# A gated linear attention and a feed-forward layer on one core: the order searched anew, some transposes moved from TensorE to transposing transfers

## The chip, the core and the metric

The kernel runs on one core of a Trainium2 chip. A core has five engines that work side by side, each through its own list in order: PE (TensorE, matmuls; PEld is its weight load), DVE (VectorE), ACT (ScalarE), POOL (GpSimd) and SP (SyncE), which here issues every transfer between main memory (HBM) and on-chip memory (SBUF). Transfers are carried out by 16 DMA engines. TensorE writes its results to PSUM, eight banks of 512 float32 in each of 128 partitions, and DVE and ACT read them there. Engines wait for each other through semaphores.

The metric is the device time of one execution in microseconds (us), lower is better, as the median of the runs.

## What is computed

```python
# r, k, v, w: [4, 8, 768, 48]   u: [8, 48]
state = zeros(B, H, D, D)
for t in range(S):
    cur = einsum('bhd,bhe->bhde', u * k[t], v[t])
    y[t] = einsum('bhd,bhde->bhe', r[t], state + cur)
    state = w[t][..., None] * state + einsum('bhd,bhe->bhde', k[t], v[t])
x = y.transpose(0, 2, 1, 3).reshape(3072, 384)

h = x @ w_in                                  # 384 -> 1024
e = exp(h - max(h)); sm = e / (sum(e) + 1e-9)
solu = h * sm
ln = (solu - mean(solu)) / sqrt(var(solu) + 1e-6) * g_ln
out = ln @ w_out                              # 1024 -> 384, float32
```

The first half is a recurrence over 768 steps with a decay w per step and channel, for 4 batches and 8 heads of 48 channels. The second half is a feed-forward layer whose hidden vector is multiplied by its own softmax and then normalised.

## The kernel before

**Units.** The time axis is cut into 6 chunks of 128 steps; a unit is one chunk of one batch, all heads: 24 units, numbered chunk first, so units 4c to 4c+3 are chunk c of the four batches. All sums over steps within a chunk become matmuls.

**Stages of one unit i**, with the words that name them in the order:

- LW, LK, LR, LV: SP loads w, k, r and v, each 128 x 8 x 48 float32, 192 KB, into rings of 7 buffers.
- lw (ACT): the logarithm of w. cum (PE): sums of it along the steps, once up to a step and once from it. ex (ACT): exponential of both, in PSUM. kp (DVE): these factors times k and r, as bfloat16, written side by side in a row of 2 x 8 x 64 = 1024.
- krk, krr (PE): four transposes each, so that the channels of two heads lie across the partitions, first for k, then for r; kr (ACT or DVE): the copy of the 128 x 1024 result from PSUM to kr_s.
- M (PE): products of k and r, 8 heads; m (DVE with the mask, or ACT followed by POOL's sel): the copy with the part above the diagonal cleared.
- p, q, qh (POOL), dg (DVE), dv (POOL): the bonus term with u, per head a sum of r k u times v. qh first halves the sum's length. vb casts v to bfloat16.
- Y (PE): attend, that is M times v, and r times the state of the chunks before. With "i" it also adds dv, by a matmul with the identity; with "n" y's copy on DVE adds it. y (ACT or DVE): the copy to bfloat16.
- S (PE), et (ACT), st (DVE): the state for the next chunk. Units of one batch are bound by it: Y and S of unit i need st of unit i-4.
- X (PE): three transposes of y; xT (ACT or DVE): the copy.
- H (PE): the hidden layer, 8 x 3 matmuls with 128 columns, w_in as the stationary side, so that hidden channels lie across the partitions. e (ACT): its exponential. he (DVE): h times e. hq (ACT or DVE): its square. ea (POOL): the sum of e's two halves, in some units.
- Oa, Ob (PE): for each of 8 blocks of hidden channels, he times w_out (385 columns, the last gives the sum of he), e or ea times a column (the sum of e), and hq times a column (the sum of squares). g_ln and the centring are put into w_out at the start (gw, mn, mc, ce).
- sq (ACT), qm (DVE): square of the sums and the variance. lv (ACT): two instructions, Ln and Exp, that make the factor of the norm. o (ACT or DVE): the product with it. out (SP): the store, 192 KB.

**Order.** Everything is laid out by one long string, ORDER (lines 21 to 67). Its words are carried out from first to last; a word is a stage and a unit, and behind a dot stands the engine (a, d, p) or the PSUM bank (0 to 7). The class InOrder makes each engine issue its instructions in just this order, so a waiting instruction holds back everything behind it on its engine, and SP's list of transfers is one such queue. The semaphores follow from which buffers are written and read. The word hot is a run of matmuls on zeros that keeps TensorE's clock up.

The loop at the end of the kernel reads the string:

```python
    for word in ORDER.split():
        word, _, how = word.partition(".")
        name = word.rstrip("0123456789")
        stages[name](int(word[len(name):]), how)
```

Since every instruction is made through the same helper, the profile gives line 86 for nearly all; groups are told apart by the names of the tiles that they write and read.

Of the kernel before, what the change touches and what calls it, by code (L numbers as in the profile page):

```python
# [8 lines left out]
F32 = mybir.dt.float32  # L9
BF16 = mybir.dt.bfloat16  # L10
# [10 lines left out]
ORDER = """  # L21
LW2 LU0 ik0 lw2 hot5.4 cum2.0 LW1 lw1 us0.7 ih0 LW3 lw3 cum3.2 LR2 uc0 ex2 LK2 p2 LV2 vb2.p kp2 hot4.4 krk2.6 krr2
LR1 LK1 cum1.4 LW0 ex1 kp1 kr2.d hot1.0 S2.7 lw0 et2 LV1 vb1.d LW4 st2 p1 q1 hot2.0 krk1.1 krr1 q2 qh2 dg2 LG0
kr1.a M2.4 ex3 hot1.0 M1.6 m1.d dv2 LR0 LK0 p0 q0 cum0.0 ex0 lw4 cum4.6 ex4 kp0 krk0.1 krr0 LR3 gs0.0 gc0 dg1
m2.d Y2.i0 kr0.d LK3 p3 LR4 LV0 vb0.a dg0 dv1 kp3 Y1.i5 hot3.1 krk3.4 krr3 LK4 kp4 M0.2 m0.d krk4.1 y1.a X1.5
krr4 y2.a X2.0 dv0 xT2.d hot1.6 Y0.n7 y0.d kr3.a M3.2 hot1.0 X0.6 S1.4 p4 q3 kr4.a xT1.a xT0.a LI2 LI1 wi1.a
M4.0 m4.a et1 LI0 S0.5 et0 wi0.d m3.d LO1 wi2.p H1.6 e1 gw5.a H2.0 e2 H0.2 LO0 gw2.a q4 qh4 dg4 qh3 dg3 gw4.p
gw7.p LV3 vb3.p dv3 sel4 LW6 e0 gw6.d st1 LV4 vb4.p he1 lw6 dv4 gw1.d LW5 gw0.d gw3.d mn0.4 mc0 ce5.p ce6.p
Y3.i7 ce4.p he2 st0 he0 cum6.0 y3.a ce7.p hot1.5 X3.6 lw5 xT3.a ce3.d LK6 LR6 p6 Y4.n5 LR5 LK5 ce2.d hq0.a ex6
LW7 cum5.2 H3.6 p5 y4.d ex5 ce1.d ce0.d Oa0.5 kp6 krk6.1 krr6 S4.0 hq1.d Oa1.4 kp5 krk5.3 krr5 X4.2 Ob1 e3 he3  # L30
LV5 q6 q5 kr5.d hq2.a et4 st4 M5.6 kr6.a M6.0 xT4.d lw7 cum7.2 hq3.a sq1 m6.a m5.d dg5 vb5.d qm1 dv5 Ob0 ex7 sq0
qm0 S3.7 qh6 LR7 LK7 p7 kp7 et3 lv1 st3 lv0 H4.0 Y5.n6 y5.d LR9 LK8 o1.d e4 krk7.3 krr7 Oa2.2 he4 X5.7 q7 kr7.d
LW9 lw9 o0.a LK9 p9 LW8 lw8 S5.6 et5 cum9.4 ex9 Ob2 sq2 LR8 p8 st5 dg6 kp9 qm2 LV6 xT5.a LV9 vb6.p dv6 sel6
cum8.0 ex8 kp8 hq4.a LV7 LV11 out1 LW10 dg7 vb7.p dv7 Oa3.3 vb9.a lv2 H5.6 e5 M7.4 m7.d he5 q8 krk9.1 LK10 krr9
kr9.a S9.0 et9 Ob3 sq3 st9 q9 qm3 o2.a out0 ea5.p Y6.i5 y6.a LV8 LR10 Y7.n4 y7.d LW11 LW12 krk8.1 M9.6 lw10 lv3
X6.2 xT6.a m9.d o3.a krr8 LV10 out3 out2 kr8.d qh9 dg9 dg8 hq5.d cum10.4 ex10 kp10 S6.0 vb11.d et6 X7.2 xT7.a
st6 p10 vb8.d dv8 dv9 H6.6 e6 he6 H7.2 lw11 e7 he7 M8.4 m8.a Oa5.1 Y9.n0 Ob5 sq5 y9.d cum11.6 ex11 krk10.5 krr10
qm5 kr10.d S7.4 et7 st7 Oa4.3 hq6.d lv5 lw12 o5.a X9.2 sel8 Y8.i0 vb10.p y8.a LK11 LR11 kp11 xT9.d q10 dg10 p11
M10.4 m10.a sel10 S10.1 et10 st10 dv10 S8.0 et8 S11.7 et11 X8.6 xT8.a LK12 LW13 cum12.4 q11 ex12 lw13 st11 st8
Ob4 sq4 qm4 LW14 LR12 kp12 p12 lw14 lv4 o4.a out5 LK13 LV12 LR13 Y10.n2 dg11 y10.d H8.6 e8 krk12.1 krk11.0 krr11  # L40
krr12 kr12.d he8 kr11.a q12 qh12 cum13.4 H9.2 vb12.p S12.1 ex13 p13 q13 ea7.p dg12 kp13 dv11 LW16 LR14 LK14 e9
he9 et12 st12 M12.6 m12.a Oa6.0 X10.5 xT10.a krk13.4 krr13 kr13.a M11.6 m11.d ea8.p dv12 sel12 p14 cum14.2 ex14
q14 out4 Ob6 sq6 hq8.d M13.4 m13.d LV13 hq7.a LW15 lw15 lw16 kp14 vb13.d H10.6 dg13 qm6 LW18 lw18 Y11.n1 y11.d
Oa8.5 LK16 LR15 LR16 LK15 e10 he10 hq9.a krk14.4 Y12.i3 krr14 lv6 qh14 kr14.d p15 ea10.p dv13 LR18 LV14 vb14.p
q15 qh15 LK18 p18 Ob8 sq8 qm8 y12.a S13.2 et13 st13 o6.a lv8 X11.1 xT11.d cum16.6 ex16 X12.3 hq10.d LW19 kp16
Oa9.4 cum15.0 xT12.a Ob9 ex15 kp15 sq9 o8.a dg14 dv14 qm9 M14.2 m14.a sel14 krk16.7 Oa7.6 krr16 kr16.d lv9 o9.d
cum18.0 ex18 kp18 Ob7 LV15 S14.5 et14 st14 krk15.3 krr15 kr15.d LK19 Y13.i2 lw19 cum19.0 krk18.7 p16 q16 vb15.a
S15.4 y13.a sq7 qm7 dg15 X13.5 xT13.d ex19 LR19 kp19 lv7 o7.a q18 krr18 kr18.d H11.2 et15 st15 krk19.5 krr19
kr19.d LW17 lw17 cum17.0 e11 he11 ex17 ea11.p out8 LK17 LR17 p17 kp17 H12.6 e12 he12 hq11.a p19 H13.4 e13 Oa10.3
Y14.n2 M16.0 m16.a dg16 q19 dv15 y14.d ea12.p ea13.p M15.6 m15.d he13 Ob10 sq10 X14.2 out9 Oa11.1 LW20 qm10 lw20  # L50
cum20.6 hq12.d krk17.0 krr17 out6 out7 LV16 vb16.a dv16 xT14.a S16.2 LR20 ex20 LK20 dg18 et16 st16 lv10 o10.a
H14.4 e14 kp20 Ob11 sq11 kr17.d LK23 qm11 lv11 o11.a Oa12.2 krk20.3 krr20 kr20.a he14 sel16 Y16.n7 y16.d Y15.n6
y15.d M19.4 m19.a M18.0 m18.d Ob12 X15.7 xT15.a q17 hq13.d LV19 LW21 LV17 X16.3 xT16.a ea14.p vb19.a M17.4 m17.d
sq12 LK22 out10 qm12 dg17 qh19 vb17.p sel19 p20 hq14.a LW22 LV20 q20 qh20 dv17 M20.0 LV21 m20.d out11 LK21 H15.6
e15 he15 lw22 ea15.p H16.4 LV18 vb18.p dv18 LR21 p21 lw21 Oa14.3 Y17.n1 LR22 LV23 q21 dg19 dv19 Ob14 LR23 p23
p22 e16 he16 lv12 Oa13.0 LW23 o12.a out12 sq14 qm14 hq15.d vb20.a lv14 dg20 dv20 y17.d cum21.6 ex21 Ob13 cum22.4
sq13 ex22 LV22 vb22.p ea16.p o14.d out14 Y18.n2 y18.d Oa15.1 X18.3 qm13 kp22 lv13 xT18.d X17.2 xT17.a kp21 Ob15
sq15 qm15 S18.5 et18 st18 Y19.n4 y19.d lv15 o15.a out15 o13.a krk22.2 S17.3 et17 lw23 H18.6 e18 ea18.p hq16.d
vb21.d st17 Y20.n5 y20.d X19.4 xT19.d krr22 kr22.a H17.0 he18 hq18.d cum23.4 ex23 kp23 Oa16.3 e17 ea17.p he17
krk21.2 krr21 kr21.a H19.6 e19 krk23.5 X20.4 krr23 q22 qh21 vb23.p out13 xT20.a kr23.a he19 Oa18.2 Ob16 sq16  # L60
M21.0 q23 ea19.p qh23 dg22 dv22 m21.a sel21 qm16 lv16 M22.6 hq19.a M23.4 Ob18 sq18 dg21 H20.0 o16.a out16 m22.d
m23.d Oa19.7 Y22.n6 qm18 lv18 hq17.d Ob19 S19.5 dg23 dv23 e20 Oa17.4 y22.d X22.3 he20 et19 st19 xT22.d dv21
Y21.n6 Ob17 y21.d sq19 o18.a sq17 qm17 lv17 Y23.n1 out18 qm19 lv19 X21.0 xT21.d H22.2 o17.a e22 out17 ea20.p
y23.d H21.0 X23.5 xT23.a e21 hq20.d o19.d out19 Oa20.6 he22 hq22.d H23.4 e23 he21 hq21.d Ob20 sq20 qm20 lv20
o20.a out20 ea22.p Oa22.7 ea21.p Oa21.3 he23 hq23.d Ob22 sq22 qm22 lv22 Ob21 sq21 qm21 lv21 o21.d o22.a out22
out21 ea23.p Oa23.2 Ob23 sq23 qm23 lv23 o23.a out23
"""

NIO, NLW, NKP, NWK = 7, 10, 6, 4
# [24 lines left out]
def kernel(  # L94
# [60 lines left out]
    g_rows = consts.tile([KF, 128], F32)  # L155

# [57 lines left out]
    qm_t = ring("qm", NWK, [C, 1], F32)  # L214
    lv_t = ring("lv", NWK, [C, 1], F32)
# [164 lines left out]

    def scores(i, x):
        kr = kr_s[i % NKP]
        m_ps = live[i]["m_ps"] = bank([C, 2, HP, C], F32, x, "m_ps")
        for hp in range(HP):
            for a in range(2):
                rows = slice(64 * a, 64 * a + 64)
                pe.matmul(m_ps[:, a, hp, :], lhsT=kr[rows, hp, :], rhs=kr[rows, HP + hp, :], start=True, stop=True)
# [80 lines left out]

    def hidden(i, x):
        xT = xT_t[i % NWK]  # L470
        h_ps = live[i]["h_ps"] = bank([128, KF, C], F32, x, "h_ps")
        for f in range(KF):
            for j in range(KM):
                pe.matmul(h_ps[:, f, :], lhsT=win_sb[:, j, f * 128:(f + 1) * 128], rhs=xT[:, j, :],
                          start=(j == 0), stop=(j == KM - 1))

    def hidden_exp(i, x):
        act.activation(out=e_t[i % NWK], in_=live[i]["h_ps"], func=EXP)
# [7 lines left out]
    def hidden_mul(i, x):  # L486
        dve.tensor_mul(out=he_t[i % NWK], in0=live[i]["h_ps"], in1=e_t[i % NWK])

    def hidden_square(i, x):
        he, hq = he_t[i % NWK], hq_t[i % NWK]  # L490
        if x == "a":
            act.activation(out=hq, in_=he, func=SQUARE)
        else:
            (dve if x == "d" else pool).tensor_mul(out=hq, in0=he, in1=he)

    def output(i, part):
        L = live[i]
        e, he, hq, o_ps = e_t[i % NWK], he_t[i % NWK], hq_t[i % NWK], L["o_ps"]
        for f in range(part * KF // 2, (part + 1) * KF // 2):
            pe.matmul(o_ps[:, :DM + 1], lhsT=he[:, f, :], rhs=w2[:, f, :], start=(f == 0), stop=False,  # L500
# [16 lines left out]

    def sums(i, x):
        act.activation(out=sq_t[i % NWK], in_=live[i]["o_ps"][:, DM:DM + 2], func=SQUARE)

    def variance(i, x):
        dve.tensor_sub(out=qm_t[i % NWK], in0=live[i]["o_ps"][:, DM + 2:], in1=sq_t[i % NWK][:, 0:1])

    def scale(i, x):
        act.activation(out=lv_t[i % NWK], in_=sq_t[i % NWK][:, 1:2], func=LN, scale=1e-6 * DF * DF,
                       bias=qm_t[i % NWK])
        act.activation(out=rs_t[i % NWK], in_=lv_t[i % NWK], func=EXP, scale=-0.5)
# [8 lines left out]
    def store(i, x):  # L536
# [11 lines left out]
        sq=sums, qm=variance, lv=scale, o=scaled_out, out=store,  # L548
# [35 lines left out]
```

## Time and profile before

| | us |
|---|---|
| median of 3 runs (155.18 to 155.82) | 155.33 |
| span of the profiled execution, first to last instruction | 152.4 |
| PE busy, 2093 matmuls | 136.4 |
| DVE busy, 227 instructions | 131.8 |
| ACT busy, 247 instructions | 120.0 |
| POOL busy, 149 instructions | 119.0 |

The span leaves out what lies before the first and behind the last instruction, 2.9 us against the median. 27.06 MB go through the DMA engines. The largest groups of the page (engine, operation, written tile <- read tiles, shape, count | busy us, mean ns of one):

| group | count | busy us | mean ns |
|---|---|---|---|
| PE, ps<-w,he, 385 columns (Oa, Ob) | 192 | 44.5 | 325 |
| PE, ps<-xT,win_sb, 128 columns (H) | 576 | 35.5 | 219 |
| PE, ps<-one_col,hq, 1 column (Oa, Ob) | 192 | 31.5 | 164 |
| PE, ps<-ident,kp, 128 columns (krk, krr) | 192 | 16.5 | 227 |
| PE, ps<-ident,y, 128 columns (X) | 72 | 7.6 | 219 |
| DVE, he<-ps,e, 128 x 1024 | 24 | 29.1 | 1214 |
| DVE, hq<-he, 128 x 1024 | 15 | 13.4 | 890 |
| ACT, hq<-he, 128 x 1024 | 9 | 9.5 | 1055 |
| ACT, kr<-ps, 128 x 1024 | 11 | 11.1 | 1012 |
| DVE, kr<-ps, 128 x 1024 | 13 | 8.9 | 682 |
| POOL, ea<-e, 128 x 512 | 17 | 20.0 | 1181 |

A matmul's shown length runs from its start to its modelled end, and the next one starts well before that; the price of one in a row of many is the step from start to start. The same holds for the busy time of PE: it counts the stretches in which at least one is under way.

### The profile page before, as it was taken

The page shows a single profiled execution, that of the slowest core. Times are in us where ns is not written, and L with a number is a line of the kernel's source. Part 1 is how long each engine was busy: PE and PEld are TensorE (multiplying, and loading weights), DVE is VectorE, ACT ScalarE, POOL GpSimd, SP SyncE. Part 2 cuts the span into 40 slices and gives each one's busy share as a digit, 9 for nine tenths or more (in the row PEclk, how much of TensorE's full clock was granted, in tenths as well). Part 3 has the DMA queues.
Part 4 walks back from the last instruction along what each step waited for, and adds up shares of the span by engine and source line. Part 5 has one row for each costly group of instructions (what it writes and reads, how often), then busy time and mean ns, then how long its engine had stood idle before and what let it go on. Part 6 is the DMA issues. An engine that isn't in the chain of part 4 may idle for free.

```text
span 152.4 us, 5172 instructions
## 1 busy us (share of the span) xinstructions
PE 136.4 (90%) x2093; PEld 105.5 (69%) x2093; DVE 131.8 (87%) x227; ACT 120.0 (79%) x247; POOL 119.0 (78%) x149
## 2 busy tenths in 40 slices
PE   6777598968999999999998999999799999999970
PEld 1242365936778889779776689887686988889740
DVE  5029968899999999998999999999999999988940
ACT  4526648869888999799998889998988789938661
POOL 7268986799909994899999997799889979973600
PEclk9959969999999999999999999999999999999998
DMA  3999999989979999989897989995998110112023
GB/s 76 218 216 211 217 334 377 254 175 223 216 151 216 220 204 229 206 177 224 194 203 144 228 195 275 199 199 136 241 205 210 63 45 4 44 63 103 4 79 127
DMA packets 104825, 27.06 MB, mean 178 GB/s; under 512 B 100314, under 2 KB 104419, under 8 KB 104803
## 3 DMA queue, kind: packets, MB, share of 16 engines
q1 hardware_dynamic: 104802, 26.75, 77.4%
q8 instruction: 16, 0.26, 0.7%
q14 instruction: 7, 0.05, 0.1%
HBM read 22.03 MB, written 4.72 MB: 176 GB/s over the span
## 4 chain that ended last, share of the span: by engine, by line
PE 53%; DVE 23%; SPq 8%; ACT 6%; issue 3%; DMA 2%; POOL 1%; DVEq 0%; POOLq 0%
PE ps L86 53%; SPq L86 7%; DVE he L86 6%; DVE m L86 4%; DVE kp L86 4%; DVE w L86 3%; DMA kr_in<-in_k_dram 2%; DVE kr L86 1%; DVE hq L86 1%; DVE y L86 1%; DVE st L86 1%; ACT ps L86 1%; ACT o L86 1%; DVE dg L86 1%; ACT win_sb L86 1%
## 5 line engine op out<-in xcount | busy, mean ns | idle before, releaser
L86 PE MATMUL ps<-w,he 128*128 128x385 bf16 x192 | 44.5, 325 | 1.0 <-DVE w L86 0.7
L86 PE MATMUL ps<-xT,win_sb 128*128 128x128 bf16 x576 | 35.5, 219 | 1.1 <-DVE qm L86 0.8
L86 PEld LDWEIGHTS <-win_sb 128*128 128x128 bf16 x576 | 32.8, 98 | 2.2 <-DVE m L86 0.9
L86 PE MATMUL ps<-one_col,hq 128*128 128x1 bf16 x192 | 31.5, 164 | 0.0
L86 DVE TENSOR_TENSOR he<-ps,e 128x1024 bf16<-128x1024 f32 x24 | 29.1, 1214 | 1.6 <-ACT e L86 1.6
L86 DVE TENSOR_TENSOR kp<-ps,kr_in 128x768 bf16<-128x768 f32 x24 | 22.8, 951 | 7.7 <-DMA kr_in<-in_k_dram 4.9
L86 POOL TENSOR_TENSOR p<-kr_in 128x384 bf16<-128x384 f32 x24 | 24.7, 1038 | 4.5 <-DMA kr_in<-in_k_dram 4.2
L86 POOL TENSOR_TENSOR dv<-vb,dg 128x384 bf16<-128x384 bf16 x24 | 21.7, 907 | 7.5 <-DVE qm L86 3.6
L86 ACT ACTIVATE e<-ps 128x1024 bf16<-128x1024 f32 x24 | 24.5, 1021 | 3.1 <-PE ps L86 2.0
L86 POOL TENSOR_TENSOR ea<-e 128x512 bf16<-128x512 bf16 x17 | 20.0, 1181 | 6.4 <-ACT e L86 5.7
L86 POOL TENSOR_TENSOR q<-p,u_bc 128x384 bf16<-128x384 bf16 x24 | 22.2, 931 | 2.4 <-DVE dg L86 1.7
L86 ACT ACTIVATE ps<-ps 128x768 f32<-128x768 f32 x24 | 19.1, 799 | 5.1 <-PE ps L86 4.3
L86 PEld LDWEIGHTS <-kp 128*128 128x128 bf16 x272 | 17.5, 100 | 6.0 <-DVE kp L86 3.2
L86 PEld LDWEIGHTS <-he 128*128 128x128 bf16 x192 | 18.4, 96 | 4.0
L86 PEld LDWEIGHTS <-hq 128*128 128x128 bf16 x192 | 15.4, 96 | 8.3
L86 DVE TENSOR_TENSOR m<-ps,keep 128x1024 bf16<-128x1024 f32 x15 | 18.2, 1216 | 1.2 <-PE ps L86 1.0
L86 PE MATMUL ps<-ident,kp 128*128 128x128 bf16 x192 | 16.5, 227 | 1.6 <-POOL p L86 1.1
L86 DVE TENSOR_TENSOR hq<-he 128x1024 bf16<-128x1024 bf16 x15 | 13.4, 890 | 0.1
L86 ACT COPY kr<-ps 128x1024 bf16<-128x1024 bf16 x11 | 11.1, 1012 | 2.4 <-PE ps L86 2.4
L86 ACT ACTIVATE lw<-w_in 128x384 bf16<-128x384 f32 x23 | 11.7, 523 | 1.3 <-DMA w_in<-in_w_dram 1.3
L86 PEld LDWEIGHTS <-kr 64*128 64x128 bf16 (+1 forms) x272 | 10.2, 95 | 3.1 <-ACT kr L86 0.7
L86 PE MATMUL ps<-inv_col,ea 128*128 128x1 bf16 x68 | 11.2, 165 | 0.0
(90 smaller groups left out, 293.7 us busy)
## 6 DMA issues: line engine op xcount, KB each, us to landing
w_in<-in_w_dram SPq DMA_DIRECT2D x24, 192.0 KB, 3.7
kr_in<-in_r_dram SPq DMA_DIRECT2D x24, 192.0 KB, 3.7
kr_in<-in_k_dram SPq DMA_DIRECT2D x24, 192.0 KB, 3.7
v_in<-in_v_dram SPq DMA_DIRECT2D x24, 192.0 KB, 3.6
out_dram<-o SPq DMA_DIRECT2D x24, 192.0 KB, 2.6
win_f<-in_moe_w_in_dram SPq DMA_DIRECT2D x3, 512.0 KB, 6.4
wout_f<-in_moe_w_out_dram SPq DMA_DIRECT2D x2, 768.0 KB, 9.0
u_row<-in_u_dram SPq DMA_DIRECT2D x1, 1.5 KB
```

Source lines behind the costliest of these rows:

```text
L86: made = make(*args, **kwargs)
```

## The change

The string ORDER is replaced as a whole: the order of all stages, the engine of those that can run on two, and the PSUM banks are other ones. Three stages get a second form, and one is split:

- In units 14 and 16 to 23, krk, krr and kr are replaced by kt: one transfer, issued by SP, that turns the 128 x 1024 row block of kp into kr_s.
- In units 12, 16 and 18 to 23, X and xT are replaced by xt, which turns y (128 x 384) into xT.
- In units 12, 14, 16 to 19, 21 and 23, H is computed the other way round, with xT as the stationary side and 512 columns of w_in at a time, so that the steps lie across the partitions. The sum of e and the sum of squares then come from the ACTIVATEs that make e and hq, as sums along the row, and Oa and Ob hold the 385-column matmuls alone. he is written to one of four buffers in the space of the float32 w_in, and ht turns it (128 x 1024) by a transfer into the form that Oa needs. sv squares the sum of e; the scale in lv changes since the sum is no longer divided by the root of 1024.
- lv is Ln alone, and Exp becomes a word of its own, rs.

Counts that change, before and after: krk and krr 24 and 15; X 24 and 16; hq on ACT 9 and 19, on DVE 15 and 5; kr on ACT 11 and 6, on DVE 13 and 9; xT on ACT 15 and 12, on DVE 9 and 4; y on ACT 7 and 2, on DVE 17 and 22; attend with dv by matmul 7 and 2; ea 17 and 11; qh 12 and 8; o on ACT 19 and 16, on DVE 5 and 8; sel 9 and 10; vb on ACT 6 and 7, on DVE 6 and 3, on POOL 12 and 14. Of the weights' preparation, one cast of w_in moves from DVE to ACT, two gains move from DVE to ACT and one centring from DVE to POOL. The warm-up runs go from 19 matmuls to 37: 13 at the start, three times 4, 2, and 10 ahead of M1.

In the new string SP's list begins LW1 LW2 LV0 LK2 LW0 LR0 LK1 LR1 LK0; the weights LI and LO stand behind 26 loads (18 before), and its last part reads: kt21 kt20 xt19 LR22 LK22 ht14 out9 kt23 ht12 out11 LV21 kt22 xt16 out13 LV23 xt18 out8 LV22 ht17 out15 xt21 LV20 ht19 xt23 ht16 ht18 out12 out14 xt22 xt20 ht21 ht23, then the last eight stores.

```diff
+    ht_t = [win_f.rearrange("p a n -> p (a n)")[:, j * DF // 2:(j + 1) * DF // 2].bitcast(BF16) for j in range(NHT)]
...
+    def turned_kr(i, x):
+        sp.dma_start_transpose(out=kr_s[i % NKP], in_=kp_t[i % NKP].rearrange("t a h d -> t (a h d)"))
+
+    def turned_x(i, x):
+        sp.dma_start_transpose(out=xT_t[i % NWK], in_=y_t[i % NWK])
+
+    def turned_he(i, x):
+        sp.dma_start_transpose(out=he_t[i % NWK], in_=ht_t[i % NHT])
...
+    by_rows = {int(word[2:].split(".")[0]) for word in ORDER.split() if word.startswith("ht")}
+
     def hidden(i, x):
         xT = xT_t[i % NWK]
+        if i in by_rows:
+            h_ps = live[i]["h_ps"] = bank([C, 2, 512], F32, x, "h_ps")
+            for j in range(KM):
+                for n in range(2):
+                    pe.matmul(h_ps[:, n, :], lhsT=xT[:, j, :], rhs=win_sb[:, j, n * 512:(n + 1) * 512],
+                              start=(j == 0), stop=(j == KM - 1))
+            return
...
     def hidden_exp(i, x):
+        if i in by_rows:
+            act.activation(out=flat(e_t[i % NWK]), in_=flat(live[i]["h_ps"]), func=EXP, accum_out=be_t[i % NWK])
+            return
...
     def hidden_mul(i, x):
+        if i in by_rows:
+            dve.tensor_mul(out=ht_t[i % NHT], in0=flat(live[i]["h_ps"]), in1=flat(e_t[i % NWK]))
+            return
...
     def hidden_square(i, x):
         he, hq = he_t[i % NWK], hq_t[i % NWK]
-        if x == "a":
+        if i in by_rows:
+            act.activation(out=flat(hq), in_=ht_t[i % NHT], func=SQUARE, accum_out=s2_t[i % NWK])
+        elif x == "a":
...
         for f in range(part * KF // 2, (part + 1) * KF // 2):
+            if i in by_rows:
+                pe.matmul(o_ps[:, :DM + 1], lhsT=he[:, f, :], rhs=w2[:, f, :], start=(f == 0), stop=(f == KF - 1))
+                continue
...
+    def spread(i, x):
+        act.activation(out=sq_t[i % NWK][:, 1:2], in_=be_t[i % NWK], func=SQUARE)
...
     def scale(i, x):
-        act.activation(out=lv_t[i % NWK], in_=sq_t[i % NWK][:, 1:2], func=LN, scale=1e-6 * DF * DF,
-                       bias=qm_t[i % NWK])
+        act.activation(out=lv_t[i % NWK], in_=sq_t[i % NWK][:, 1:2], func=LN,
+                       scale=1e-6 * DF if i in by_rows else 1e-6 * DF * DF, bias=qm_t[i % NWK])
+
+    def root(i, x):
         act.activation(out=rs_t[i % NWK], in_=lv_t[i % NWK], func=EXP, scale=-0.5)
```

## The prediction, made before the changed kernel was built or run

> **What bounds the kernel now.** I read four views, in this order: the busy times and the chain of waits, to find the engine that sets the end; the windows, stage by stage; the timeline of TensorE, for the price of each step; and the transfers after 118 us, for the room that the new ones would use.
>
> ```profile
> span 152.4 us, 5172 instructions
> PE 136.4 (90%) x2093; PEld 105.5 (69%) x2093; DVE 131.8 (87%) x227; ACT 120.0 (79%) x247; POOL 119.0 (78%) x149
> ...
> 43.27 31.86 PE ps L86 x551
> ...
> 83.53 6.06 PE ps L86 x79
> ...
> 110.34 37.23 PE ps L86 x601
> ```
>
> The last three rows are pieces of the chain (start, length, what). From 43 to 75 us and from 110 us to the end TensorE sets the time without a gap; between 75 and 110 us the chain hops mostly between DVE instructions. So two engines bind in turn. The windows (columns: engine busy, granted clock, share of the 16 DMA engines, GB/s) show who stands close behind:
>
> ```profile
> 43.30:75.10 31.80, 31.80 (x554) 26.39 (x554) 30.82 (x54) 29.30 (x66) 26.20 (x32) 1.00 0.96 204
> 75.10:110.30 35.20, 33.67 (x563) 27.39 (x560) 34.63 (x54) 32.27 (x67) 32.98 (x35) 1.00 0.95 201
> 110.30:147.60 37.30, 37.23 (x601) 30.14 (x601) 33.97 (x58) 28.90 (x68) 27.52 (x30) 1.00 0.30 82
> ```
>
> The DMA engines are full (0.95) until the last load has gone and nearly empty (0.30) in the stretch that TensorE alone decides. ACT has 8.4 us of room there, DVE 3.3 us. The prices on TensorE come from starts, since a matmul's shown length includes its pipeline:
>
> ```profile
> 119.83 1.50 PE L86 MATMUL ps<-xT,win_sb 128*128 128x128 bf16 x24
> 121.17 0.33 PE L86 MATMUL ps<-st,kr 128*128 128x96 bf16 x4
> ...
> 121.55 0.33 PE L86 MATMUL ps<-ident,y 128*128 128x128 bf16 x3
> 121.72 0.39 PE L86 MATMUL ps<-ident,kp 128*128 128x128 bf16 x4
> 121.94 1.50 PE L86 MATMUL ps<-xT,win_sb 128*128 128x128 bf16 x24
> ...
> 123.75 0.33 PE L86 MATMUL ps<-w,he 128*128 128x385 bf16 x1
> 123.92 0.17 PE L86 MATMUL ps<-inv_col,ea 128*128 128x1 bf16 x1
> 123.95 0.16 PE L86 MATMUL ps<-one_col,hq 128*128 128x1 bf16 x1
> 123.97 0.32 PE L86 MATMUL ps<-w,he 128*128 128x385 bf16 x1
> ```
>
> The hidden product (H) takes 121.17-119.83 = 1.34 us, the three transposes of y (X) 0.17 us, four of k or r 0.22 us (eight: 0.45 us), a 385-column matmul 0.17 us and each one-column matmul behind it 0.025 us: the next 385-column one starts 0.22 us after the last, 0.05 us of it for two of them.
>
> **The change on TensorE.** Nine units lose krk and krr: 9 x 0.45 = 4.1 us. Eight lose X: 8 x 0.17 = 1.4 us. Eight compute H by rows and lose the eight hq and four ea columns of the output product: 12 x 0.025 = 0.30 us; their six 512-column matmuls pass the same 3,072 columns as the 24 of 128 did, at 0.165/385 us a column 1.30 us, 0.04 us less; together 8 x 0.34 = 2.7 us. The matmul that adds dv inside attend goes from 7 units to 2: 5 x 0.165 = 0.8 us. Units that sum e by eight columns instead of ea's four go from 7 to 5: 0.2 us. Sum: 9.2 us less, nearly all in units 12 to 23, where TensorE sets the end.
>
> Warm-up matmuls go from 19 to 37. TensorE's other work starts as loads arrive (busy 33.7 of the first 43.3 us), so I cost the 18 at nothing; if that cover fails, the ten ahead of M1 cost 10 x 0.22 to 0.43 = 2 to 4 us (0.43 us is the step of the first four, 1.91/4 with the last one's pipeline off).
>
> **On the other engines,** by the rows' means. DVE: ten hq fewer (890 ns), four kr (682), five xT (349), one m, three vb (635), one win_sb, two gains, one centring less; five y (551) and three o (610) more, four sums over 384 instead of 192 columns: -14.0 us, to about 118. ACT: ten hq more (1,055 ns: +10.6), five kr (1,012: -5.1), three xT (-1.4), five y (-2.4) and three o (-1.7) less, one m, one vb, one win_sb and two gains more (+3.7), eight 1-column squares (sv, 170 ns: +1.4). Sixteen ACTIVATEs also give a sum along the row, which no row shows: between nothing and one smallest instruction (170 ns) each, 0 to 2.7 us, and I take 1.6, nearer the middle. ACT: +6.7, to about 127. POOL: six ea (1,181) and four halvings (548) less, one mask, two casts, one centring more: -6, to 113. Ln and Exp apart change no duration: back to back they stood 0.03 us apart (148.00 + 0.30, then 148.32), so at most 24 x 0.03 us of ACT, nothing on the path.
>
> So TensorE 127, ACT 127, DVE 118: three near-equal engines, all at work in order. **How much of 9.2 us arrives?** In the stretch 75 to 110 us, where three engines were near full together, TensorE lost 35.20-33.67 = 1.5 us, 4.3%. I expect that loss over the 75 us or so in which they now run together: 3.3 us. It is an estimate; its bounds are 0 (43 to 75 us: no loss) and 7 us (double).
>
> **The transfers** are the unknown. 25 enter SP's queue: 17 of 256 KB (nine of kp, eight of he) and eight of 96 KB (y), and each waits in the queue for DVE or ACT to have written its source. Behind kt14 stand three loads of units 16 and 18; behind kt19, 16, 17 and 18 the stores out6, out7, out4 and the loads of v19 and w23; behind xt19 the loads of k and r of unit 22; behind xt21 that of v20, which POOL needs for vb20 and dv20, so Y20 waits for it. The room:
>
> ```profile
> DMA  0001900000000000060023004700000140083600
> ...
> out_dram<-o SPq DMA_DIRECT2D x10, 192.0 KB, 1.8
> ```
>
> These are the transfers from 118 us on: an almost empty machine, and a 192 KB store lands 1.8 us after its issue. No row shows a transposing transfer. By engine time: the loads move 192-byte pieces, 104,802 packets for 77.4% of 16 x 152.4 us, so 18.0 ns each; a 128 x 1024 tile turned in runs of 128 elements (256 B) is 1,024 such pieces, 64 per engine: 1.15 us. Low end, at the rate of the store: 0.7 us. High end, if one is wholly done before the next begins, at the loads' 3.7 us for 192 KB: 4.9 us. I take 1.15 us, the row with the nearest piece size, and 1.8 + 1.15 = 3 us to land.
>
> The Trainium skill, "DMA: Bandwidth & Descriptors", section "Latency and other measured facts", gives 261 GB/s for a transposing transfer; by that a 256 KB one takes 1.0 us and the sum is the same. Against the change speaks "VectorE: DVE Perf Modes", section "The three transpose paths": 1,309 ns by transfer for 128 x 128 against 390 ns on TensorE; the trace's 55 ns steps there are far below its 390, and eight blocks one after the other would take 10.5 us, beyond my high end.
>
> Where they fall: from ht14 on, the order lists ten large and six small ones, seven stores and four loads ahead of the last (ht23), and 23.5 us of TensorE work at the prices above. A small one counts 0.375 of a large, a plain issue 0.39 us: 12.25 x 1.15 + 4.3 = 18.4 us. It fits, with 5 us to spare. It ceases to fit at (23.5-4.3)/12.25 = 1.6 us each.
>
> **Forecast.** 152.4 - 9.2 + 3.3 = 146.5 us of span; the 2.9 us between the span and the median of the runs (155.33) stay: 149.4, say 149.5 us; own range 147.5 to 152.
>
> **Rivals.**
> A. Everything arrives: no loss by crowding, 152.4 - 9.2 + 2.9 = 146.1 us. For: 43 to 75 us ran without a gap. Against: ACT now has as much work as TensorE.
> B. ACT becomes the bound: it was 28.3 of the first 43.3 us at work; with 127 us in all, 15 lost at the start and 3.6 at the end the span is 145.6 at best, a median of 148.5, and at 95% in between 152.3, a median of 155.2; the upper part, 153 to 156, is this rival. For: hq goes to it. Against: its work is spread more evenly.
> C. Late loads: those behind waiting transposes come late for the last attends, 2 to 5 us: 151.5 to 154.5. For: the four v loads stand among the last ten transposes. Against: the DMA engines are idle there.
> D. The other side: transposes run one behind the other, in SP's queue or in the engines, and TensorE waits at the late M, H and Oa. Each large one costs x; the end slips by 12.25x + 4.3 - 23.5 us. It decides from x = 2.0 us (slip 5.8, the gain gone); at x = 3.0, midway between my value and the high end, the slip is 17.5: 167 us; at 4.9, 40.8: 190 us. For: plain issues already hold SP for 0.4 to 1.0 us under load, and between ht23's issue and Oa23 there are only 2.7 us of TensorE work, less than my 3 us to land. Against: stores of nearly that size land in 1.8 us. The skill's 1,309 ns a block would be beyond even 190.
> E. That the turned units' work isn't less on TensorE I give nothing: the instructions are gone from the code.
>
> **Chances.** Forecast 0.44, A 0.11, B 0.12, C 0.03, D 0.30 (0.06 of it at the far end). A measurement of this kernel tells about 0.5% (0.8 us) from no change. Faster: 0.44 + 0.11 + 0.05 of B + 0.02 of C = 0.62. Within 0.5%: 0.05 of B + 0.01 of C = 0.06. Slower: 0.30 + 0.02 of B = 0.32. Range 145.5 to 166: the top is D with x = 2.9; left out are 0.03 below and some 0.15 of D.
>
> **What would show it.** TensorE busy near 127 plus 4 to 7 us of warm-ups; ACT near 127, DVE near 118; kp transposes x120 instead of x192. Transposing transfers landing within 3 to 4 us, SP's waits no longer than now, and TensorE without gaps from 45 us on confirm the forecast. It is wrong if rows such as "PE waits for DMA kr, xT or he" hold more than 3 us, if the interval between successive transposes in SP's queue is above 1.6 us where their sources were long ready, or if ACT stands in the chain for more than a tenth of the span.

## The result and the profile after

The changed kernel takes 167.69 us (median of 4 runs, 165.03 to 168.37) against 155.25 us for the kernel before in runs beside it (154.22 to 155.82). Executions of one kernel fall into a faster and a slower state, and all times and ratios from here on are those of the fast runs, for the changed kernel 166.22 us, 1.0719 times as long as the kernel before, with a 95% interval of 1.0609 to 1.0829. It is slower, and above the top of the predicted range (166 us). The profiled execution took 167.97 us, its span 165.8 us.

The page of the changed kernel: busy times, DMA row (40 slices of 4.1 us), the queue of the transfers, and the shares of the chain of waits.

```profile
span 165.8 us, 4574 instructions
PE 133.9 (81%) x1756; PEld 94.8 (57%) x1762; DVE 118.8 (72%) x208; ACT 123.0 (74%) x270; POOL 110.2 (66%) x143
...
DMA  5999999998989997997999989998989978895443
...
q1 hardware_dynamic: 126082, 32.00, 91.9%
...
DMA 30%; SPq 19%; PE 16%; ACT 15%; issue 8%; POOL 7%; DVE 2%; DVEq 0%; POOLq 0%; ACTq 0%
```

TensorE, DVE and POOL have less to do than before, ACT has 3.0 us more, and the span is 13.4 us longer. The DMA row no longer falls at three quarters of the span: the DMA engines stay nearly full to 149 us. TensorE's share of the chain is 16% (before 53%); DMA and SP's queue have 49% (before 10%). Total time of the 16 DMA engines, from the share of the queue: before 77.4% of 152.4 = 118.0 us, now 91.9% of 165.8 = 152.4 us.

The windows of the changed kernel, with the same limits as those shown of before (columns: engine busy, granted clock, DMA share, GB/s):

```profile
43.30:75.10 31.80, 28.11 (x459) 23.12 (x457) 29.11 (x46) 27.72 (x57) 26.73 (x30) 1.00 0.94 193
75.10:110.30 35.20, 31.26 (x505) 23.75 (x506) 28.31 (x46) 29.99 (x67) 33.03 (x39) 0.97 1.04 197
110.30:147.60 37.30, 30.33 (x340) 19.05 (x343) 26.40 (x44) 29.87 (x75) 18.78 (x23) 0.99 0.96 181
```

In the last stretch the DMA share went from 0.30 to 0.96, and TensorE from 37.2 us busy to 30.3. It is no longer the engine that decides there, and nothing on ACT or DVE is full either.

The transfers of the changed kernel (tile views: the time for which SP's queue holds one, lowest, median, highest in ns; when the first and last are issued), then its transfer view from 118 us on (KB, median us from issue to landing):

```profile
L84 SPq DMA_TRANSPOSE kr<-kp x9: 1305/1828/2499, 77.4 to 128.3; - x9
...
L84 SPq DMA_TRANSPOSE he<-win_f x8: 1248/1258/2527, 122.1 to 151.7; - x8
...
L84 SPq DMA_TRANSPOSE xT<-y x8: 1182/1210/1613, 112.0 to 149.0; - x8
```

```profile
DMA  9963999998974777992993909923998003814080
...
out_dram<-o SPq DMA_DIRECT2D x15, 192.0 KB, 2.2
v_in<-in_v_dram SPq DMA_DIRECT2D x4, 192.0 KB, 3.4
...
he<-win_f SPq DMA_TRANSPOSE x8, 3.1
xT<-y SPq DMA_TRANSPOSE x7, 2.4
kr<-kp SPq DMA_TRANSPOSE x4, 4.5
```

The k and r transfers begin at 77 us, far ahead of the "almost empty machine" that the prediction showed for 118 us on, and that machine is no longer empty: loads of v are still among them. SP's queue in the changed kernel (start, length, what; the length of a row of several includes the gaps):

```profile
95.15 0.70 SPq L84 DMA_DIRECT2D w_in<-in_w_dram  x1
...
99.72 7.35 SPq L84 DMA_TRANSPOSE kr<-kp  x4
107.16 1.50 SPq L84 DMA_DIRECT2D out_dram<-o  x3
108.72 0.45 SPq L84 DMA_DIRECT2D v_in<-in_v_dram  x1
...
115.59 3.85 SPq L84 DMA_TRANSPOSE kr<-kp  x2
...
139.34 0.57 SPq L84 DMA_DIRECT2D v_in<-in_v_dram  x1
```

The row at 95.15 us is the 81st of the 96 loads. Up to there the changed kernel is not behind: in the kernel before, the 81st load's issue ends at 97.2 us. The issue of the last load ends at 139.9 us instead of 115.2. So the 15 last loads take 44 us where they took 18. Between them stand eight k and r transfers, five of y and three of he, 11 large and 5 small ones.

That alone does not make the transfers the cause. In no_turns, the changed order without any of them (an experiment below), the same 15 loads take 41 us, from the end of the first of these two issues to the end of the second:

```profile
93.44 0.82 SPq L84 DMA_DIRECT2D w_in<-in_w_dram  x1
...
135.05 0.43 SPq L84 DMA_DIRECT2D v_in<-in_v_dram  x1
```

SP's queue stands still there in front of stores whose source is not written yet. So the late places of the last loads belong to the new order; what differs is how full the DMA engines are meanwhile and who waits. The longest waits for transfers in the changed kernel (engine, tile, releaser: us in total, times, longest), and then POOL's wait for v in no_turns:

```profile
POOL vb L84 <- DMA v_in<-in_v_dram: 16.6, 9, 2.9
...
PEld L84 <- DMA he<-win_f: 5.8, 4, 2.2
PE ps L84 <- DMA he<-win_f: 4.0, 3, 1.8
```

```profile
POOL vb L84 <- DMA v_in<-in_v_dram: 3.5, 3, 2.9
```

From 60 us on POOL waits 13.7 us for v in the changed kernel and 0.4 us in no_turns. (DVE's wait for r, 9.1 us in all, and ACT's for w, 6.7 us, lie ahead of 60 us but for 0.9 us each, and stand in no_turns too, with 8.3 and 5.1 us.) TensorE's matmuls wait 4.0 us for he, and 2.0 us once for kr; the row of PEld shows the same waits for he at the weight load, so the two don't add up. What TensorE loses to late loads of v reaches it through POOL.

The chain of waits that ended last (start, length, what) has 16.1 us of landings of transposing transfers behind 100 us, and 3.3 us of a load's:

```profile
102.01 5.06 DMA kr<-kp
...
121.47 3.32 DMA kr_in<-in_k_dram
...
135.81 3.54 DMA he<-win_f
...
140.01 3.25 DMA he<-win_f
...
144.02 4.21 DMA he<-win_f
```

To follow the time, I split the span into TensorE's work without warm-ups and the rest (waiting and warm-ups), by the windows 0 to 50, 50 to 100, 100 us to the end. The warm-ups (ps<-warm rows) take 7.8 us of busy time before and 10.9 after.

| us | work 0-50 | 50-100 | 100-end | sum | rest 0-50 | 50-100 | 100-end | sum |
|---|---|---|---|---|---|---|---|---|
| before | 32.6 | 49.2 | 46.8 | 128.6 | 17.4 | 0.8 | 5.6 | 23.8 |
| after | 27.6 | 46.1 | 49.4 | 123.1 | 22.4 | 3.9 | 16.4 | 42.7 |
| after_half | 30.1 | 50.0 | 43.0 | 123.1 | 19.9 | 0.0 | 10.2 | 30.1 |
| no_turns | 27.6 | 47.7 | 58.2 | 133.5 | 22.4 | 2.3 | 10.6 | 35.3 |

(after_half and no_turns are experiments, below.) TensorE did lose 5.5 us of work. The rest grew by 18.9 us: 5.0 at the start, 3.1 in the middle, 10.8 at the end. Of that, 11.5 us (5.0, 1.5 and 5.0) stand in no_turns as well, without a transfer.

### The profile page after: what moved, and what is told of

It is laid out like the page before. It is cut to its first block, busy times and chain, and to the rows that moved or that the text cites. A ratio compares the mean times of both kernels' runs of the same rounds, so it can differ in the third digit from the quotient of the medians.

```text
span 165.8 us, 4574 instructions
## 1 busy us (share of the span) xinstructions
PE 133.9 (81%) x1756; PEld 94.8 (57%) x1762; DVE 118.8 (72%) x208; ACT 123.0 (74%) x270; POOL 110.2 (66%) x143
## 3 DMA queue, kind: packets, MB, share of 16 engines
q1 hardware_dynamic: 126082, 32.00, 91.9%
## 4 chain that ended last, share of the span: by engine, by line
DMA 30%; SPq 19%; PE 16%; ACT 15%; issue 8%; POOL 7%; DVE 2%; DVEq 0%; POOLq 0%; ACTq 0%
SPq L84 18%; PE ps L84 16%; DMA he<-win_f 7%; DMA w_in<-in_w_dram 5%; DMA kr_in<-in_k_dram 5%; ACT e L84 4%; DMA win_f<-in_moe_w_in_dram 3%; DMA kr<-kp 3%; DMA v_in<-in_v_dram 3%; DMA out_dram<-o 2%; DMA kr_in<-in_r_dram 2%; ACT ps L84 2%; POOL m L84 2%; POOL q L84 2%; ACT lw L84 2%
## 5 line engine op out<-in xcount | busy, mean ns | idle before, releaser
L84 PE MATMUL ps<-xT,win_sb 128*128 128x128 bf16 x384 | 23.3, 219 | 2.3 <-DVE kp L84 1.8
L84 PEld LDWEIGHTS <-win_sb 128*128 128x128 bf16 x384 | 22.1, 98 | 3.4 <-issue 2.1
L84 PE MATMUL ps<-one_col,hq 128*128 128x1 bf16 x128 | 21.0, 164 | 0.0
L84 POOL TENSOR_TENSOR dv<-vb,dg 128x384 bf16<-128x384 bf16 x24 | 19.9, 832 | 1.7 <-DVE dg L84 0.8
L84 DVE TENSOR_TENSOR he<-ps,e 128x1024 bf16<-128x1024 f32 x16 | 19.3, 1218 | 1.9 <-ACT e L84 1.2
L84 POOL TENSOR_TENSOR ea<-e 128x512 bf16<-128x512 bf16 x11 | 12.7, 1157 | 10.0 <-ACT e L84 10.0
L84 POOL CAST vb<-v_in 128x384 bf16<-128x384 f32 x14 | 7.1, 505 | 16.7 <-DMA v_in<-in_v_dram 16.6
L84 DVE TENSOR_TENSOR st<-ps,et 128x384 bf16<-128x384 f32 x20 | 10.9, 550 | 4.2 <-ACT et L84 4.0
L84 DVE TENSOR_TENSOR y<-ps,dv 128x384 bf16<-128x384 f32 x22 | 12.0, 549 | 2.5 <-PE ps L84 2.0
L84 PE MATMUL ps<-ident,kp 128*128 128x128 bf16 x120 | 11.3, 240 | 3.0 <-DVE kp L84 2.1
L84 PEld LDWEIGHTS <-hq 128*128 128x128 bf16 x128 | 10.4, 96 | 5.7 <-issue 0.2
```

What stands on the lines that cost most here:

```text
L84: made = make(*args, **kwargs)
```

## The experiments

All ratios are to the kernel before, run beside on the same chip, with the 95% interval.

### Undoing the transfers, one kind at a time and all

no_turns puts TensorE's transposes back for all 25; no_kt, no_xt and no_ht undo only those of k and r, of y, or of he. The order of all else stays.

```diff
-kt14
+krk14.2 krr14 kr14.a
...
-xt12
+X12.1 xT12.a
...
-ht14
-sv14
```

> All 25 transposing transfers are undone in the changed order (krk, krr, kr, X, xT, and H by columns again; the copies go to ACT and DVE in turn). Theory 1 (two losses: before 100 us the new order stands about 8 to 10 us of TensorE work behind, and after 100 us the transposes on SP's queue cost the rest): 158 to 163 us. Rival 2 (the transposes are the whole loss): 153 to 157 us. Rival 3 (the order alone is the loss, the transposes gain what was hoped): 172 us or more.

> Only the nine kt are undone (17.6 us of SP's time in the profile, at 1.3 to 2.5 us each, six of them ahead of loads). Theory 1: the largest part of what the transposes cost is here, since loads stand behind them: 161 to 164 us. Rival 2: 158 to 161 us. Rival 3: 170 us, as TensorE gets 4 us more.

> Only the eight xt are undone (about 10 us of SP's time at 1.2 us each, for 1.4 us of TensorE work). If SP's time per transfer whatever its size is what counts, this helps nearly as much per transfer as undoing ht: 162 to 165 us. If bytes in the DMA engines count, it helps little: 165 to 167 us.

> Only the eight ht are undone (about 11 us of SP's time, 8 x 256 KB, 2.7 us of TensorE work). TensorE waits 10 us for their landing in the profile. Theory 1: 161 to 165 us. Rival 3: 168 us or more.

| | median us | ratio |
|---|---|---|
| changed kernel | 166.22 | 1.0719 (1.0609 to 1.0829) |
| no_kt | 163.93 | 1.0543 (1.0452 to 1.0633) |
| no_xt | 162.94 | 1.0485 (1.0400 to 1.0571) |
| no_ht | 165.42 | 1.0638 (1.0538 to 1.0738) |
| no_turns | 171.15 | 1.1026 (1.0955 to 1.1096) |

Without one kind the kernel is 0.8 to 3.3 us faster (only no_xt's interval stands clear of the changed kernel's), without all three 4.9 us slower. Of the three expectations for no_turns the first two failed by 8 us or more; 171 us is nearest to the third, that the order alone is the loss and the transfers gain. In this order they do gain, 4.9 us on balance. The parts don't add up, as if they shared something, and what is taken out of it first helps until another bound is reached. The window of no_turns shows that other bound:

```profile
100.00:168.80 68.80, 58.20 (x922) 47.29 (x921) 44.84 (x77) 48.70 (x108) 28.77 (x35) 0.97 0.33 89
```

The DMA share is 0.33, close to the 0.30 before the change, and TensorE has 58 us of work left at 100 us. The transfers remove 133.5-123.1 = 10.4 us of TensorE's work from this order and return 42.7-35.3 = 7.4 us of it as waiting. And the changed order without any transfer is 16 us slower than the order before. It may have been made for units that are cheap on TensorE late; no run shows that, and how far my places for the restored stages add to these 16 us isn't known.

### Lighter loads

after_half and before_half load four of the eight heads for units 7 and up. The other heads keep what the buffer held, so the output is no longer the layer's. All instructions of the other engines stay. If the transfers' trouble is that they share the DMA engines with the loads, it should go.

```diff
+    def loaded(i):
+        return H if i < NIO else H // 2
...
-        sp.dma_start(out=w_t[i % NIO][:, :, :D], in_=rows_of(w, i))
+        sp.dma_start(out=w_t[i % NIO][:, :loaded(i), :D], in_=rows_of(w, i)[:, :loaded(i), :])
```

> The changed kernel, but from unit 7 on each load of w, k, r and v brings 4 of the 8 heads (the other half stays what the buffer held), so 6.7 MB less go through the DMA engines and every instruction stays. Theory 1a (the DMA engines are full, loads and transposes land late): the 3 us lost between 50 and 100 us and most of the 11 us lost after it come back, 152 to 157 us. Theory 1b (SP's issue time per transposing transfer, 1.2 us whatever its size, holds the queue): 162 us or more. The start (5 us) stays lost in both.

> The same cut of the loads in the kernel before, as the control: its TensorE has no gaps after 43 us, so 153 to 155 us under every theory; a gain of over 3 us would say that the loads bound it too.

The changed order falls from 166.22 to 153.59 us (0.9948, 0.9900 to 0.9996); the order before doesn't gain, with 155.47 us (1.0077, 1.0045 to 1.0109). The kernel before wasn't held up by the size of its loads, the changed one is, by 12.6 us. Windows of after_half:

```profile
50.00:100.00 50.00, 50.00 (x869) 40.55 (x865) 48.12 (x81) 48.92 (x108) 48.75 (x58) 1.00 0.67 133
100.00:153.20 53.20, 42.98 (x469) 27.83 (x466) 36.26 (x60) 39.50 (x107) 25.16 (x30) 0.96 0.71 153
```

From 50 to 100 us TensorE now works without a gap, as the forecast had it from 45 us on. no_turns_half then took the transfers out with the loads light as well:

> The changed order with all transposing transfers undone, as in no_turns (171.2 us), and the loads halved from unit 7 on. If the order without the transfers is held by loads: 160 us or less. If it is held by TensorE's work and the places at which the undone stages stand: 166 us or more, that is, the transfers were worth their TensorE time to this order and only the DMA engines spoil it.

It takes 168.77 us (1.0882, 1.0828 to 1.0937). So light loads are worth 171.15-168.77 = 2.4 us where no transfer competes and 166.22-153.59 = 12.6 us where 25 do. With light loads the transfers save 168.77-153.59 = 15.2 us, with full ones 4.9. The 10.2 us between are what loads and transfers cost together in this order, but not all of it is shown to be the sharing of the engines. By the table after_half has done 6.4 us more of TensorE's work by 100 us (80.1 against 73.7), and up to 99 us the changed kernel has issued a single transposing transfer, kt14. And no_turns has 10.4 us more work for TensorE, behind which late loads can hide.

### Smaller transfers

In after_small each transposing transfer turns only 128 columns (32 KB) of its tile; the rest of its target keeps old values.

```diff
-        sp.dma_start_transpose(out=he_t[i % NWK], in_=ht_t[i % NHT])
+        sp.dma_start_transpose(out=he_t[i % NWK][:, 0, :], in_=ht_t[i % NHT][:, :C])
```

> The changed kernel, but each of the 25 transposing transfers turns only 128 of its columns (the rest of its target keeps old data), an eighth or a third of the bytes; waits and order stay. Theory 1a: the 33 us that the transposes take of the engines go, 156 to 160 us. Theory 1b: SP still needs about 1.2 us for each, 164 us or more.

> The changed kernel with both cuts: half the bytes of the loads from unit 7 on, and 128 columns for each transposing transfer. after_half was 154.6 us, with TensorE still waiting 9 us for the landing of he. If that rest is bandwidth: 149 to 152 us, near the forecast. If it is the time of a transfer to land, which depends little on its size (2.3 against 2.7 us), or the order itself: 153 to 155 us.

after_small takes 159.53 us (1.0331, 1.0267 to 1.0394): 6.7 us less than the changed kernel. The number of transfers and their places in SP's queue are the same, and SP holds a small one of he nearly as long as a large one (tile view and transfer view of after_small):

```profile
L83 SPq DMA_TRANSPOSE he<-win_f x8: 1172/1184/1682, 119.3 to 146.1; - x8
```

```profile
he<-win_f SPq DMA_TRANSPOSE x8, 2.3
```

1.18 us at 32 KB against 1.26 us at 256 KB. All 25 hold SP for 35.3 us against 38.7, 3.4 us less, while the 16 DMA engines' time for them falls from 34.4 to 4.3 us (76.3% of a span of 160.3 us, less 118.0). So most of the 6.7 us is the time in the DMA engines, not SP's. With the loads light too, after_half_small takes 153.78 us (0.9894, 0.9823 to 0.9965) against after_half's 153.59: where the engines have room, the size hardly matters, and of the 3.1 us that he takes to land 2.3 are there at 32 KB too.

### A transfer that nobody waits for, early and late

before_spare_mid adds to the kernel before nine transfers of 256 KB between the 60th and the 92nd load. They turn a tile that was long ready into space that nobody reads, so that no engine's work and no wait for data changes. before_spare_tail has the same nine behind the last load.

```diff
+    def turned_spare(i, x):
+        into = spare[:, (1 + i % 5) * DF:(2 + i % 5) * DF].rearrange("p (a n) -> p a n", a=KF)
+        sp.dma_start_transpose(out=into, in_=win_sb[:, 0, :])
```

> The kernel before, with nine extra transposing transfers of 256 KB (a fixed tile into the unused w_in buffer, nothing waits for them) behind the loads no. 60, 64, ... 92, where the DMA engines are 0.95 busy. No work of an engine changes. If the engines' time is the price (1.7 us each by the packets of the changed kernel): the loads end about 15 us later and the kernel takes 162 to 170 us. If only SP's issue counts and has room: 156 us or less.

> The kernel before with nine extra transposing transfers of 256 KB as in before_spare_mid, but all behind the last load (one behind v22's load, two each behind H17, H19, H20 and H22). If a transposing transfer costs nothing where the DMA engines and SP are idle: 154 to 155.5 us, against 163.5 us in the full stretch. If it disturbs TensorE's or DVE's memory accesses: 157 us or more.

Early they cost 9.1 us: 163.51 us (1.0583, 1.0542 to 1.0624). Late they cost nothing: 154.80 us (0.9992, 0.9955 to 1.0030). The queue of before_spare_mid, and that of before_spare_tail (packets, MB, share of 16 engines' span):

```profile
span 162.6 us, 5179 instructions
...
q1 hardware_dynamic: 114306, 29.11, 82.2%
```

```profile
span 153.4 us, 5182 instructions
...
q1 hardware_dynamic: 114306, 29.11, 86.7%
```

82.2% of 162.6 less the 118.0 us of the kernel before is 15.7 us, 1.74 us for each; 86.7% of 153.4 gives 15.0 and 1.67. In the changed kernel it is (152.4-118.0)/20 = 1.72 us, a small one counted 0.375. Three runs give one price, half as much again as the 1.15 us that I took. But the price alone decides nothing: paid in the full stretch it delays the loads behind it (the last one goes out at 126.6 us instead of 114.8, and the engines' share is 1.0 until then), paid behind the last load it is free. SP holds each of the nine for 1.4 to 3.6 us in before_spare_mid, so this run by itself doesn't tell SP's time from the engines'; after_small does.

### The order before, with as many transfers as it bears

Transfers in place of TensorE's transposes where the order before has them: four (kt21, kt22, xt19, xt20, all behind the last load), six (with ht17 and ht20), eight (with xt17 and ht16, these two ahead of late loads).

```diff
-X19.4 xT19.d
+xt19
...
-krk21.2 krr21 kr21.a
+kt21
```

> The order before, with four transposing transfers that all stand behind the last load in SP's queue: kt 21 and 22, xt 19 and 20. TensorE loses 0.9 + 0.34 = 1.2 us, ACT two copies of kr. In before_turns8 the transfer of he16 held v22's load back by 4.6 us. If that hold in SP's queue was the harm there: 153 to 154.5 us. If a transposing transfer costs by itself: 155.5 us or more.

> The order before with six turned stages behind the last load: kt 21 and 22, xt 19 and 20, ht 17 and 20. TensorE loses 0.9 + 0.34 + 0.68 = 1.9 us, ACT gains two squares, two reads of the sum and two sv (2 x 1.7 us) and loses two copies of kr (2 us), DVE loses two squares. If TensorE's work is all that counts in that stretch: 152.5 to 153.5 us. If the landing of 2.7 us stands ahead of Oa20 (4.8 us between source and use) or ACT's work holds it: 154 to 155.5 us.

> The order before, with eight transposing transfers where SP and the DMA engines are idle and at least 4.8 us lie between source and use: kt 21 and 22, xt 17, 19 and 20, ht 16, 17 and 20, each issued right behind its source. TensorE loses 2 x 0.45 + 3 x 0.17 + 3 x 0.34 = 2.4 us in the stretch that it bounds alone. If transposing transfers are harmless where the queue is free: 152.5 to 153.5 us. If they cost by themselves: 155 us or more.

| | median us | ratio |
|---|---|---|
| before_turns4 | 154.02 | 0.9974 (0.9931 to 1.0018) |
| before_turns6 | 156.36 | 1.0105 (1.0056 to 1.0154) |
| before_turns8 | 156.68 | 1.0148 (1.0092 to 1.0203) |

Four change nothing that can be told; six and eight make it slower, by 1.0 and 1.5%. SP's queue in before_turns8, and then in the kernel before:

```profile
112.16 1.19 SPq L84 DMA_DIRECT2D kr_in<-in_r_dram  x1
115.48 1.32 SPq L84 DMA_TRANSPOSE he<-win_f  x1
116.86 0.58 SPq L84 DMA_DIRECT2D w_in<-in_w_dram  x1
...
119.42 0.59 SPq L84 DMA_DIRECT2D v_in<-in_v_dram  x1
```

```profile
114.78 0.43 SPq L86 DMA_DIRECT2D v_in<-in_v_dram  x1
```

SP issues nothing from 113.35 to 115.48 us: ht16 waits there for DVE's product in the space of win_f (its row starts at 114.25 us and takes 1.21), and the load of w behind it waits with it; the last load goes out 4.6 us later than before. That is rival C of the prediction in one place. In before_turns6, which has no such transfer, the chain from 129 us on runs mostly through ACT (hq, e and o) where in before_turns4 it is one piece of TensorE:

```profile
126.84 21.01 PE ps L84 x333
```

There the hq that row sums move from DVE to ACT seem to be what costs; that is read from the chain, and no run took it apart. No complete version was faster than the kernel before by more than its interval.

### The weights and the start

before_late_w pulls eight loads ahead of the weights in the order before (behind 26 loads instead of 18); after_early_w puts the weights behind 18 in the changed one.

```diff
-xT0.a LI2 LI1
+xT0.a LV3 LW6 LV4 LW5 LK6 LR6 LR5 LK5 LI2 LI1
...
-LV2 cum4.4
+LV2 LI0 LO1 LI1 LI2 LO0 cum4.4
```

> The kernel before, with one edit: the five loads of w_in and w_out stand behind 26 loads of w, k, r and v instead of 18, as in the changed kernel. If the later weights are what costs the changed kernel its 5 us at the start: 160 to 164 us (eight loads of 0.95 us ahead of them, 7.6 us, less what TensorE can do meanwhile). If they are harmless: 156 us or less.

> The changed kernel with the five loads of weights moved up to stand behind 18 loads, as before. If the weights' lateness is the loss at the start: 162 to 165 us. If it is the order of TensorE's work (it has the attention of seven units ahead of H, whose loads now come later): 167 us or more.

before_late_w takes 162.78 us (1.0529, 1.0494 to 1.0565), 8.4 us more; after_early_w 168.37 (1.0901, 1.0856 to 1.0946), 2.2 us more than the changed kernel. Here the queue and the order fit each other: either one moved alone costs. Then two kernels that begin as the kernel before does, for its first 184 or 289 words, and go on in the changed order with all that is left:

```diff
-LW1 LW2 lw2 LV0 LK2 LW0 hot13.0 cum2.0 ex2
+LW2 LU0 ik0 lw2 hot5.4 cum2.0 LW1 lw1 us0.7
```

> The first 184 words of the order before (the start, to about 38 us of its profile), then all that is left in the changed order, transposing transfers included. If the 5 us at the start come from the changed order's first part: 160 to 163 us. If the loss only moves (the rest was laid out for its own start): 166 us or more.

> The same with the first 289 words of the order before (to about 66 us), then the changed rest. If the start and the waits for loads up to 66 us are the changed order's own: 158 to 161 us; what is left above 154.5 us is then the price of the second half with its 25 transposing transfers, most of it DMA engine time.

168.82 us (1.0889, 1.0821 to 1.0957) and 166.93 us (1.0785, 1.0710 to 1.0859). splice289 has TensorE busy for 40.5 of the first 50 us, as before the change (38.4 in the changed kernel), and gains nothing: it then has 40.0 busy from 50 to 100 us, where the changed kernel has 46.1. The start's loss is real, but mending it alone doesn't move the end: the loss comes back between 50 and 100 us, and no run shows why.

## Why the prediction was wrong

**The step that failed is "The transfers", with the comparison under "Where they fall".** It set 18.4 us of transfers against 23.5 us of TensorE work from ht14 on, took the DMA engines for almost empty, and so put what the transfers cost the loads and TensorE at nothing. By after_small their size alone costs 6.7 us. Place and size were wrong in it, and beside it the new order itself stood at nothing.

*The place.* Nine of the 25 stand ahead of ht14: kt14, kt16 to 19, xt12, kt21, kt20, xt19. They aren't in the comparison. At the measured 1.72 us, seven large and two small ones are 7.75 x 1.72 = 13.3 us of engine time, put into a stretch whose share I had shown as 0.95. The other sixteen don't meet an almost empty machine either: the share from 110 to 148 us is 0.96, where it was 0.30. The end of the loads, 140 us instead of 115, is late in no_turns too (135 us), but there the engines have room meanwhile (0.33 from 100 us on). after_half (-12.6 us) and after_small (-6.7 us) show that loads and transfers are in each other's way, and the two spare kernels that the place decides.

*The size.* 1.72 us instead of 1.15. 21,280 packets more take 34.4 us x 16: 25.9 ns for a 256-byte piece against 18.0 ns for the loads' 192-byte pieces. I had carried the loads' price over by the piece; by the byte it would have been 24.0 ns and 1.54 us. In my own comparison 1.72 us gives 12.25 x 1.72 + 4.3 = 25.4 against 23.5 us, a slip of 1.9 us. So the size alone would have made a small miss. Both together are 15.2 us, close to the 15.6 us by which the rest exceeds the 3.3 us that I had allowed; that is luck, since 11.5 us of the growth stand in no_turns without a transfer, and nine spare transfers cost only 9.1 us for their 15.7.

*The order.* Without a transfer the changed order is 16 us slower than the order before, by no_turns. The prediction had nothing for it. How much of the 16 us comes from my places for the restored stages stays open.

The Trainium skill, "DMA: Bandwidth & Descriptors", section "Latency and other measured facts", gives 261 GB/s for such transfers with a non-contiguous middle dimension, and more for contiguous ones; 256 KB in 1.72 us are 152 GB/s here, with loads beside and nearly so without (1.67 us in before_spare_tail). The 1,309 ns a block of its "VectorE: DVE Perf Modes", section "The three transpose paths", which spoke against the change, isn't what a large one costs: eight blocks took 1.72 us of the engines, 1.26 us of SP's queue and landed after 3.1 us.

**The rivals.** D gave 167 us at x = 3.0, and 166 to 168 us came. With the measured 1.72 us D's own sum is a slip of 1.9 us, so its number is luck. (Two slips of mine in the sums: at x = 2.0 it gives 5.3, not 5.8 us; and 3,072 columns at 0.165/385 us take 1.32, not 1.30 us, 0.1 us over the eight units.) Its waits are real, though. TensorE's for he and kr are 6.0 us, above the 3 us that I had named as a sign, and the chain has 16.1 us of such landings behind 100 us. SP holds a transfer for at least 1.1 us whatever its size, and a small one counts there as a whole one, not 0.375; but after_small, with the same queue, is 6.7 us faster, so that much is mostly not SP's. C, late loads behind the transposes, had 0.03 with "the DMA engines are idle there". They are not, and POOL's waits for v are 13.7 us from 60 us on against 0.4 in no_turns; its price, 2 to 5 us, was for four v loads alone. How the loss divides between C's waits and D's, no run shows. B fell: ACT is 74% busy and 15% of the chain, above the tenth that I had named, but no window has it full. A fell with the forecast.

**What was right.** Instruction counts and engines: kp transposes x120, DVE 118.8 us (forecast 118), POOL 110.2 (113), ACT 123.0 (127). A row of the changed kernel's groups (line, engine, shape, count | busy, mean ns | idle before):

```profile
L84 ACT ACTIVATION_READ_ACCUMULATOR e<-ps 128x1 f32 x8 | 1.6, 199 | 0.0
```

A sum along the row is an instruction of its own, 0.2 us; my 0.1 was the middle of bounds that ended at 0.17.

**Half right.** TensorE's work fell by 5.5 us, not 9.2. The transfers took 10.4 us off this order, and the order had added 4.9 (133.5-128.6). A part of that may be the clock at the start: the windows of the changed kernel give (the number ahead of the DMA share is the granted clock)

```profile
20.00:30.00 10.00, 6.23 (x88) 4.76 (x88) 8.04 (x12) 4.77 (x9) 7.75 (x10) 0.80 1.00 217
30.00:40.00 10.00, 7.72 (x112) 6.20 (x109) 7.37 (x14) 8.02 (x15) 7.33 (x9) 0.69 0.98 313
```

where before had 0.91 and 1.00. The first hidden product starts at 38.6 us instead of 26.1. That the weights stand behind eight more loads is not the whole reason: so placed in the order before (before_late_w), it starts at 33.3 us, and with the weights moved up in the changed order (after_early_w) at 48.3. I had costed the start at nothing because TensorE's work "starts as loads arrive"; it costs 5.0 us by the table, and the splices show that mending it alone doesn't help. I hadn't priced the weights' place at all.

**Left open.** after_half, at 153.59 us, still is above the forecast. Its profiled execution took 155.3 us against 149.4: 3.7 us of TensorE work that didn't go, and 3.0 us more of waiting than the 27.1 forecast (23.8 + 3.3), less 0.8 us that I had added too much outside the span. These weren't separated further. Nor is the changed kernel's loss divided fully between the order, the engines' time and SP's queue. Whether another order, with transfers only behind its last load, would beat the kernel before wasn't settled: with four it is even.

## What to carry to other kernels

Before work is moved to a shared resource, sum that resource over the whole kernel, and place each new user on its timeline: a stretch that is empty now stays empty only if nothing moved in front of it delays what ends there. Nine transposing transfers were free behind the last load and cost more than half their engine time ahead of it. In an in-order queue a transfer that waits for its source holds every load behind it, 2.1 us in before_turns8 for one that was to save TensorE 0.34. And where order and method change together, run the new order without the new method before late loads are put down to it: here they were late in both.

## What the hardware showed that I had not expected

- SP's queue holds a transposing transfer for 1.1 to 1.3 us at least, nearly the same for 32, 96 and 256 KB; plain issues among them take 0.4 to 0.6 us from 120 us on.
- A transposing transfer of 256 KB adds some 1,056 packets and 1.67 to 1.74 us of all 16 DMA engines, whether loads run beside it or not.
- Its landing varies less than its size: for he 2.3 us at 32 KB (after_small) and 3.1 us at 256 KB (the changed kernel), for kr 3.6 and 4.5 us.
- Nine of them, added ahead of late loads where nobody waits for them, made a kernel 5.8% slower: 0.58 us for each us of engine time.
